# Transposing the fifth token tile's probabilities on TensorE in an attention and mixture-of-experts kernel

## The chip, the cores and the metric

One core of a Trainium2 chip runs the whole kernel. The metric is device time in microseconds, the median of several runs. The engines named here are TensorE (PE in the profile; PEld is its weight load), VectorE (DVE), ScalarE (ACT) and SyncE (SP). SyncE issues every DMA of this kernel, transposing ones too, in one queue.

## The reference

Attention with a learned bias that depends on position, and behind it a mixture of eight experts whose gate is balanced by eight Sinkhorn steps:

```python
B, H, S, D = (4, 8, 576, 64)              # E, DM, F = 8, 512, 1024
scores = q @ k^T / sqrt(D) + bias          # bias: [H, S, S], from positions
attn = exp(scores - max); attn = attn / (sum(attn) + 1e-9)
x = (attn @ v), heads side by side         # [2304, 512]
P = exp(x @ w_gate - max), then 8 times: rows and columns normalised
out = sum over e of P[:, e] * (relu(x @ w1[e]) @ w2[e])
```

## The kernel before

**Two stages.** In the first, attention runs, together with the first expert's products on those rows of x that are done; in the second, the other experts. Both write their instructions into a planner (class `Plan`) which gives each a cost, puts them into an order for each engine by a list schedule, and emits them. A DMA transpose has costs of its own in it (`transfer`, L206). Every instruction of the first stage shows line 202, the place where recorded instructions are issued, so the profile tells them apart by tile names.

**Units.** The attention works on 16 units, each of one batch and two heads. The 576 tokens of a head are cut into four tiles of 128 and a rest of 64; the rests of both heads share one tile, the unit's fifth token tile. A unit so has 9 score tiles of 128 x 576: two for each of four 128-token tiles, and one for both heads' rest. They go in five steps: four of two tiles each (`gi` 0 and 1, `hh` 0 and 1), and one step of a single tile (`gi` 2).

**A step.** `scores` multiplies q and k into a PSUM tile `ps_s` (tag s, two of them, 1024 float32 columns or two banks each). `st_max` on VectorE adds the bias, writes `sb` and takes the maximum. `st_exp` on ScalarE makes the exponentials and their sums, `st_rcp` the reciprocals. The probabilities are written as two float16 parts: `st_hi` (ScalarE) writes the high part of `ah`, `st_lo` (VectorE) the low part. `ah` is 128 x 1152 for one score tile, 128 x 2304 for two, and there are two `ah` buffers. Then `ah` is transposed, block of 128 x 128 by block, into `aT`: 18 blocks for a step of two tiles (tag aT, three buffers), 9 blocks for the fifth tile's step (tag aT4, one buffer). Before the change, `st_lo` ends in one DMA transpose, whatever the step:

```python
sync.dma_start_transpose(out=s["aT"], in_=ah.rearrange("p n s -> p (n s)"))
```

`attend` multiplies `aT` with v into the PSUM tile pv two steps later (`LAG = 2`); ScalarE and VectorE cut the product into two float16 parts of x (xa, xb, xc).

**Around it.** One pass of the main loop records, in this order: the scores of step n + 1, the exponentials of step n, the maxima of step n + 1, the value products that are due, `st_hi` and `st_lo` of step n - 1, the hooks, and one or two pieces of the first expert (tile l). The hooks load and cut the q, k and v of units to come (nat, qk, vs) and load bias tiles (bt) for SyncE's queue. `u_trans` transposes q and k on TensorE (8 blocks, 8 blocks and 2 blocks a unit) through a PSUM tile of tag l1, and copies them out as qkT. PSUM has eight banks: four for the two score tiles, two for l1, one each for l2 and pv.

Of the kernel before, what the change touches and what calls it, by code (L numbers as in the profile page):

```python
# [9 lines left out]
F16 = mybir.dt.float16  # L10
# [8 lines left out]
P = 128  # L19
# [243 lines left out]
def attention_sinkhorn_moe(ctx, tc, q, k, v, w1, b1, w2, wg, m1, m2, xm, xm4, xf, sel, out):  # L263
# [11 lines left out]
    plan = Plan()  # L275
    vec, act, pool, pe, sync = (
        Engine(plan, e, n)
        for e, n in ((nc.vector, "dve"), (nc.scalar, "act"), (nc.gpsimd, "pool"), (nc.tensor, "pe"), (nc.sync, "dma"))
    )
# [15 lines left out]
    id16 = consts.tile([P, P], F16, name="id16")  # L295
# [109 lines left out]
    with ExitStack() as actx:  # L405
# [35 lines left out]
        def ps_s():  # L441
            return psA.tile([P, 1024], F32, name="ps_s", tag="s", bufs=2)
# [68 lines left out]
        for kind in range(1, 4):  # L511
            vec.scalar_tensor_tensor(
                out=wr,
# [8 lines left out]
            out=wa.rearrange("p g (j k) -> p (g j) k", j=4),  # L522
# [88 lines left out]
        def bias_step(between=()):  # L611
# [27 lines left out]
            out=w1r, in0=pw[:, H : H + 2], scalar1=s_wb[:, 0:1], scalar2=2.0**-11, op0=ALU.mult, op1=ALU.mult  # L639
# [5 lines left out]
            out=w2m,  # L645
# [22 lines left out]
        for i in range(2):  # L668
            r = slice(32 * i, 32 * i + 1)
# [122 lines left out]
        with plan.urgent():  # L792
# [6 lines left out]
            out=c8, in0=u_qk[:, 0:1], scalar=0.125, in1=u_qk[:, 1:2], op0=ALU.mult, op1=ALU.mult  # L799
# [7 lines left out]
            out=g, in0=g0, scalar=s_qk[:, 0:1], in1=s_qk[:, 1:2], op0=ALU.mult, op1=ALU.mult  # L807
# [140 lines left out]
        def st_lo(s):  # L948
            n, ah = len(s["sb"]), s["ah"]
            s["aT"] = wrk.tile([P, 9 * n, P], F16, name="aT", tag="aT" if n == 2 else "aT4", bufs=3 if n == 2 else 1)  # L950
            for i, sb in enumerate(s["sb"]):
                vec.scalar_tensor_tensor(
                    out=ah[:, i, S:],
                    in0=sb,
                    scalar=s["st"][:, 3, i : i + 1],
                    in1=ah[:, i, 0:S],
                    op0=ALU.mult,
                    op1=ALU.subtract,
                )
            sync.dma_start_transpose(out=s["aT"], in_=ah.rearrange("p n s -> p (n s)"))  # L960

        def attend(u, gi, ss):

# [158 lines left out]
        for n in range(NS + LAG + 1):  # L1122
# [19 lines left out]
            if 0 < n <= NS:  # L1142
                s = steps[n - 1]
                st_hi(s)
                st_lo(s)
                u, gi, hh = s["key"]
                groups.setdefault((u, gi), []).append(s)
                if gi == 2 or hh == 1:
                    due.append((n + LAG, u, gi, groups.pop((u, gi))))
# [19 lines left out]
        vec, act, pool, pe, sync = nc.vector, nc.scalar, nc.gpsimd, nc.tensor, nc.sync  # L1169
# [623 lines left out]
    for n, (e, b) in enumerate(seq):  # L1793
        r = visit[n]
# [94 lines left out]
```

## Time and profile before

| what | value |
|---|---|
| median of 3 runs | 1820.13 us |
| lowest and highest run | 1817.78 and 1821.13 us |
| profiled execution | 1816.04 us, span 1814.2 us |
| TensorE busy | 1678.9 us, 93% of the span |
| VectorE busy | 1481.0 us, 82% |
| ScalarE busy | 1089.9 us, 60% |
| DMA queue of SyncE | 306496 packets, 327.51 MB, 60.6% of 16 engines' span |

The profile is of one execution, and its times are counted from the start of its span. The shares are averages over both stages, which have different limits; the attention ends at about 540 us. A wait is put down to whatever released it last.

### The profile page before, as it was taken

The page shows a single profiled execution, that of the slowest core. Times are in us where ns is not written, and L with a number is a line of the kernel's source. Part 1 is how long each engine was busy: PE and PEld are TensorE (multiplying, and loading weights), DVE is VectorE, ACT ScalarE, POOL GpSimd, SP SyncE. Part 2 cuts the span into 40 slices and gives each one's busy share as a digit, 9 for nine tenths or more (in the row PEclk, how much of TensorE's full clock was granted, in tenths as well). Part 3 has the DMA queues.
Part 4 walks back from the last instruction along what each step waited for, and adds up shares of the span by engine and source line. Part 5 has one row for each costly group of instructions (what it writes and reads, how often), then busy time and mean ns, then how long its engine had stood idle before and what let it go on. Part 6 is the DMA issues. An engine that isn't in the chain of part 4 may idle for free.

```text
span 1814.2 us, 40312 instructions
## 1 busy us (share of the span) xinstructions
PE 1678.9 (93%) x16574; PEld 1372.1 (76%) x16574; DVE 1481.0 (82%) x2748; ACT 1089.9 (60%) x1930; POOL 1.5 (0%) x10
## 2 busy tenths in 40 slices
PE   7777598899889899789999999999999999999998
PEld 4444355565566688678898898889888988898887
DVE  7999889888868788868887888778788879886666
ACT  7787678888856755555655555455556455453443
POOL 0000000000000000000000000000000000000000
PEclk9998699899999999899999999999999999999999
DMA  8768998999994234574565448455644564463321
GB/s 277 245 164 189 241 196 192 210 197 216 195 242 174 75 117 174 179 263 162 171 213 204 158 166 289 141 198 195 236 152 165 200 213 144 163 238 112 93 83 36
DMA packets 306680, 330.07 MB, mean 182 GB/s; under 512 B 191680, under 2 KB 234432, under 8 KB 301504
## 3 DMA queue, kind: packets, MB, share of 16 engines
q1 hardware_dynamic: 306496, 327.51, 60.6%
q8 instruction: 129, 2.11, 0.5%
q14 instruction: 55, 0.45, 0.1%
HBM read 195.72 MB, written 88.08 MB: 156 GB/s over the span
## 4 chain that ended last, share of the span: by engine, by line
PE 75%; DVE 10%; DMA 7%; ACT 2%; issue 2%; SPq 2%; DVEq 0%; ACTq 0%
PE bankA L1519 17%; PE bankA L1539 13%; PE bankB L1539 9%; PE bankE L1519 9%; PE bankE L1539 9%; PE l L202 5%; PE bankB L1519 4%; PE pv L202 3%; PE s L202 3%; DMA aT<-ah 2%; PE bankA L385 2%; SPq L202 2%; DVE area L202 1%; DVE sb L202 1%; DVE ah L202 1%
## 5 line engine op out<-in xcount | busy, mean ns | idle before, releaser
L1519 PEld LDWEIGHTS <-slot 128*128 128x128 f16 x5040 | 452.4, 98 | 65.3 <-issue 18.1
L1539 PEld LDWEIGHTS <-hA 128*128 128x128 f16 x2268 | 222.4, 98 | 33.8 <-issue 5.0
L202 PEld LDWEIGHTS <-area 128*128 128x128 f16 x2477 | 153.1, 99 | 108.0 <-issue 38.0
L1519 PE MATMUL bankE<-xt,slot 128*128 128x256 f16 (+1 forms) x1680 | 188.7, 264 | 10.8 <-ACT xt L1355 7.8
L1519 PE MATMUL bankA<-xt,slot 128*128 128x256 f16 (+1 forms) x1680 | 185.9, 262 | 0.4 <-ACT u L1576 0.4
L1564 ACT ACTIVATE hA<-c 128x512 f16<-128x512 f32 x189 | 117.9, 627 | 106.5 <-DVE c L1197 105.9
L1539 PEld LDWEIGHTS <-area 128*128 128x128 f16 x1512 | 148.0, 98 | 18.8 <-issue 1.4
L1539 PEld LDWEIGHTS <-hS 128*128 128x128 f16 x1512 | 147.7, 98 | 19.0 <-ACT hS L1564 1.3
L1197 DVE SCALAR_TENSOR_TENSOR hA<-c,hA 128x512 f16<-128x512 f32 x189 | 127.2, 684 | 11.5 <-ACT hA L1564 9.4
L202 DVE SCALAR_TENSOR_TENSOR ah<-sb,st,ah 128x576 f16<-128x576 f32 x144 | 113.1, 812 | 21.0 <-ACT ah L202 20.5
L1623 ACT COPY u<-bankA 128x512 f32<-128x512 f32 (+1 forms) x70 | 37.9, 542 | 153.5 <-PE bankA L1539 153.4
L202 ACT ACTIVATE ah<-sb,st 128x576 f16<-128x576 f32 x144 | 105.5, 771 | 28.4 <-DMA aT<-ah 23.0
L202 ACT ACTIVATE sb<-sb,st 128x576 f32<-128x576 f32 x144 | 110.5, 769 | 16.9 <-DVE st L202 16.6
L1576 ACT ACTIVATE u<-bankA 128x512 f32<-128x512 f32 x126 | 75.1, 596 | 73.7 <-PE bankA L1519 69.2
L202 PE MATMUL l<-area 128*128 128x512 f16 x413 | 110.0, 387 | 6.5 <-ACT area L202 2.2
L1197 DVE SCALAR_TENSOR_TENSOR acc<-c,fs,acc 128x256 f32<-128x256 f32 x252 | 110.1, 478 | 1.7
L202 PE MATMUL s<-qkT 128*128 128x512 f16 (+3 forms) x560 | 84.9, 306 | 24.6 <-DVE st L202 19.8
L1539 PE MATMUL bankB<-area,hA 128*128 128x256 f16 x756 | 90.8, 277 | 4.8 <-DVE area L1197 4.8
L1539 PE MATMUL bankA<-area,hA 128*128 128x256 f16 x756 | 88.4, 273 | 1.8 <-ACT hA L1564 1.4
L1539 PE MATMUL bankA<-area,hS 128*128 128x256 f16 x756 | 88.4, 273 | 1.4 <-ACT hS L1564 1.0
L1539 PE MATMUL bankA<-area 128*128 128x256 f16 x756 | 88.2, 273 | 1.0 <-ACT u L1623 1.0
L1539 PE MATMUL bankB<-area 128*128 128x256 f16 x756 | 88.5, 273 | 0.0
(228 smaller groups left out, 3090.2 us busy)
## 6 DMA issues: line engine op xcount, KB each, us to landing
sc_w<-stage SPq DMA_DIRECT2D x84, 512.0 KB, 3.1
acc<-sc_y SPq DMA_DIRECT2D x102, 256.0 KB, 4.0
area<-sc_w SPq DMA_DIRECT2D x48, 512.0 KB, 4.4
sc_y<-acc SPq DMA_DIRECT2D x84, 256.0 KB, 2.3
bt<-sc_bias SPq DMA_DIRECT2D x32, 576.0 KB, 4.7
xt<-sc_t SPq DMA_DIRECT2D x18, 1024.0 KB, 4.9
slot<-sc_w SPq DMA_DIRECT2D x36, 512.0 KB, 5.3
raw<-in_moe_w_dram SPq DMA_DIRECT2D x28, 512.0 KB, 4.9
```

The lines of the kernel that those rows point to most:

```text
L202: self.plan.record(self.name, cost, lambda: fn(*args, **kw), ins, outs, move)
L385: pe.matmul(ps[:, :512], h[:, a, ft, j * P : (j + 1) * P], w[:, wl, c : c + 512], start=(ft == 0 and i == 0), stop=(ft == 7 and i == 2),)
L1197: vec.scalar_tensor_tensor(out=o, in0=x, scalar=s, in1=y, op0=op0, op1=op1)
L1519: pe.matmul(ps[:, jf * w : jf * w + w], t[:, a, c * 512 + f * P : c * 512 + f * P + P], x(xp, c), start=(first and jf == 0 and c == 0 and ...
L1539: pe.matmul(ps[:, j * 256 : j * 256 + 256], h[:, a, fc * w + j * P : fc * w + j * P + P], t[:, wp, fc * 256 : fc * 256 + 256], start=(firs ...
L1564: on_act(0.58, lambda: act.activation(h[:, 0, sl], x, AF.Relu if relu else AF.Copy), [r], wk)
L1576: on_act(0.55, lambda: act.activation(tmp[k], bank[b], f, scale=HS), [b], [k], 0)
L1623: on_act(0.27 * nt, lambda: act.copy(tmp[k][:, :n], bank[b][:, :n]), [b], [k], 0)
```

## The change

The fifth token tile's step (`n == 1` score tile) no longer ends in a DMA transpose. Nine TensorE transposes write its blocks into a PSUM tile taken from the two score tiles (tag s, read as float16), recorded in the planner as one piece of work, and ScalarE copies them out to `aT`. The steps of two score tiles keep their DMA transpose.

```diff
@@ -957,7 +957,14 @@
                     op0=ALU.mult,
                     op1=ALU.subtract,
                 )
-            sync.dma_start_transpose(out=s["aT"], in_=ah.rearrange("p n s -> p (n s)"))
+            if n == 2:
+                sync.dma_start_transpose(out=s["aT"], in_=ah.rearrange("p n s -> p (n s)"))
+                return
+            ps = ps_s().bitcast(F16)[:, : 9 * P].rearrange("p (r x) -> p r x", x=P)
+            with plan.as_one():
+                for r in range(9):
+                    pe.transpose(ps[:, r], ah[:, 0, r * P : (r + 1) * P], id16)
+            act.copy(s["aT"], ps)
 
         def attend(u, gi, ss):
```

## Rows read from the trace of the kernel before

**Rows 1.** Busy time by stretch, one row a stretch, columns named in the first line

```profile
core 0: us, PE busy (x) PEld busy (x) DVE busy (x) ACT busy (x) POOL busy (x), PEclk, DMA share, GB/s
70.00:230.00 160.00, 112.06 (x1341) 67.53 (x1342) 147.45 (x303) 120.67 (x233) 0.00 (x0) 0.85 0.82 199
230.00:510.00 280.00, 254.52 (x2466) 162.66 (x2465) 245.51 (x598) 227.90 (x462) 0.00 (x0) 0.96 0.98 201
540.00:1814.20 1274.20, 1234.76 (x11641) 1090.35 (x11637) 1013.85 (x1706) 672.71 (x1106) 0.00 (x0) 0.99 0.48 169
```

**Rows 2.** Chain of waits from 230 to 510 us, shares by line

```profile
by line: PE l L202 29.9%; PE pv L202 15.5%; DMA aT<-ah 10.7%; PE s L202 9.7%; SPq L202 7.5%; issue 4.1%; DMA nat<-in_k_dram 4.0%; DVE ah L202 3.7%; DVE sb L202 3.2%; DMA nat<-in_q_dram 2.0%; ACT ah L202 1.4%; DVE area L202 1.2%; DVE qkT L20
```

**Rows 3.** Chain in order of time, start and length: two of ten transfers, and the end

```profile
286.28 6.41 DMA aT<-ah
...
478.54 2.40 DMA nat<-in_q_dram
...
504.74 6.08 DMA aT<-ah
...
535.67 4.33 PE bankS L1253 x169
```

**Rows 4.** DMA view from 230 to 510 us

```profile
DMA packets 139343, 56.37 MB, mean 201 GB/s; under 512 B 129072, under 2 KB 133936, under 8 KB 139312
...
q1 hardware_dynamic: 139312, 55.96, 97.3%
...
aT<-ah SPq DMA_TRANSPOSE x60, 5.1
```

**Rows 5.** All instructions on the tile aT, from issue to landing

```profile
DMA to landing us min/median/max: 3.2/5.0/8.5
```

**Rows 6.** SyncE's issues in order of time: start, length

```profile
316.40 2.71 SPq L202 DMA_TRANSPOSE aT<-ah  x1
...
319.83 1.32 SPq L202 DMA_TRANSPOSE aT<-ah  x1
...
460.58 1.69 SPq L202 DMA_TRANSPOSE aT<-ah  x1
...
464.36 3.92 SPq L202 DMA_TRANSPOSE aT<-ah  x1
```

**Rows 7.** Waits from 70 to 540 us: total us, times, longest

```profile
PEld L202 <- issue: 118.2, 254, 3.6
PE s L202 <- DVE st L202: 33.6, 30, 3.5
ACT ah L202 <- DMA aT<-ah: 23.0, 19, 3.0
DVE ah L202 <- ACT ah L202: 20.5, 20, 2.6
ACT sb L202 <- DVE st L202: 16.6, 20, 2.0
DVE sb L202 <- PE s L202: 12.1, 12, 1.9
```

**Rows 8.** TensorE transposes of q and k: all of them, and one group

```profile
L202 PE MATMUL l<-id,qk x288: 216/219/314, 63.1 to 489.3; 128*128 128x128 f16 x144
...
331.26 0.62 PE L202 MATMUL l<-id,qk 128*128 128x128 f16 x8 [1.98 <-DVE qk L202]
```

**Rows 9.** ScalarE copies out of PSUM by shape, up to 540 us

```profile
L202 ACT COPY qkT<-l 128x1024 f16<-128x1024 f16 x14 | 14.0, 999 | 2.9 <-PE l L202 2.7
...
L202 ACT COPY qkT<-l 128x256 f16<-128x256 f16 x14 | 5.1, 363 | 1.1 <-PE l L202 1.0
```

**Rows 10.** Two score tiles on TensorE, and one tile's maximum on VectorE

```profile
462.74 1.15 PE L202 MATMUL s<-qkT 128*128 128x512 f16 x8
...
460.47 0.81 DVE L202 CUSTOM_DVE_ANT_0 sb<-s,bt,sms 128x576 f32<-128x576 f32 x1
```

## The prediction

> **What bounds the kernel now.** I first read the busy times by stage, to see where the change can act [rows 1]. Up to 540 us the attention runs, and from there the experts. The fifth tiles all lie in the first part; in the second TensorE is busy 1234.76 of 1274.20 us and its order of work is planned by itself, so whatever the attention ends earlier or later moves the end by the same amount. I found no other way for the change to reach the second part.
>
> In the steady part of the attention (230 to 510 us) nothing is clearly the bound: of 280 us TensorE is busy 254.52, VectorE 245.51, ScalarE 227.90, and the DMA share is 0.98 [rows 1]. From 70 to 230 us VectorE leads with 147.45 of 160. So I went to the chain of waits for 230 to 510 us [rows 2]. TensorE's three lines there make 29.9 + 15.5 + 9.7 = 55.1%. Transfers make 10.7 (landing of transposes) + 4.0 + 2.0 (loads of k and q) = 16.7%, which is 46.8 us, and SP's own issuing 7.5%, 21 us. ScalarE's only line there of any size is 1.4%. The chain changes hands all the time: TensorE for some 10 us, then a late transfer, then TensorE again. Ten transfers carry the 46.8 us [rows 3]; the reader is to see that such a piece is either a transpose that took 6 us from issue to landing, or a load that SP issued late.
>
> Next the DMA view of the same stretch: the packets fill 97.3% of the 16 engines' time, 129072 of 139343 packets are under 512 bytes, and 60 transposes were issued [rows 4]. Sixty transposes are twelve units of five: 48 of 18 blocks of 128x128 and 12 of 9 blocks, 972 blocks. At 128 rows a block that is 124416 packets, which accounts for most of the small ones: the transposes fill the DMA engines in this stretch. A transpose takes 3.2 us to land at best, 5.0 at the median and 8.5 at worst [rows 5].
>
> **What is removed.** Sixteen transposes of 9 blocks. On SP such an issue takes 1.32 us in one place and 1.69 in another, against 2.7 to 3.9 of an 18-block one [rows 6]; 1.5 us x 16 = 24 us of SP's queue and, at half of what a large one costs, about as much of the DMA engines. Behind each stand in SP's queue the bias loads (bt) and the loads of q, k and v; when SP reaches the transpose before VectorE has written the tile's low part, they wait too. After the change SP comes to them at once. The fifth tile's ah buffer also comes free when TensorE has read it, not when a transfer has landed. ScalarE waits 23.0 us in 19 places for a transpose to release ah [rows 7], and the transposes of the chain end in that wait or in that of the value products. What is late next: the 64 large transposes, which stay.
>
> What this is worth has to be bounded. Above: 24 us, if the DMA engines are the true bound and every freed microsecond shortens the stage. Below: nothing, since none of the ten transfers on the chain is itself shown to be a 9-block one, so what helps is only that the others find a shorter queue. In between, in proportion: the twelve small ones are 108 of 972 blocks, or 108 x 128 = 13824 of 139343 packets, 10%; 10% of the 46.8 + 21 us on the chain is 7 us. I take more than that, because what a queue that is 97% full costs is mostly waiting: the median landing stands 1.8 us above the best. If the ten chain pieces lose half of this, they lose 9 us; with 10% of SP's 21 us (2 us) and an estimated 1 us in the stretches before and after, it is 12 us.
>
> **What is added.** TensorE: nine transposes for each of 16 tiles. The kernel has such a group already, eight transposes of the q and k parts in 0.62 us [rows 8]; nine are 0.70 us, and 16 groups 11.2 us. Below, nothing (all inside idle time, of which TensorE has 25 us in 230 to 510 us); above, 11.2 us. I take its share of the chain, 55%: 6.2 us. A single transpose of the group shows 219 ns in the trace, but they overlap: eight in 0.62 us is 78 ns each, and that is what the queue behind them sees [rows 8]. The Trainium skill, TensorE: Matmul & The Clock Gate, Part 4: PE-mode transpose, speaks against the change here: it gives about 275 ns for one in a kernel's context, which one after the other would be an estimated 2.5 us a tile and 40 us in all, and the sum below would be -12 + 22 + 0.7 = +11 us. The trace agrees with the size of one and not with their coming one after the other, so this stands among the rivals with a small chance.
>
> ScalarE: one copy of 1152 columns out of PSUM. The 1024-column copy takes 0.999 us and the 256-column one 0.363 [rows 9], so 0.83 ns a column and 1.10 us here, 17.7 us over 16 tiles. Its cover is ScalarE's idle time, 52 us in 230 to 510 us; it appears on the chain with a few per cent, I take 4%, so 0.7 us. Without the cover it would cost the 17.7. Behind a copy that waits for its transposes stand the exponentials of the next step on ScalarE, and VectorE's low part waits for those in turn.
>
> VectorE gets nothing. The landing tile aT4 has one buffer, but its reader of the unit before is a whole unit, 23 us, older, so I expect no wait there. The planner gets other costs and may order all engines differently; that I can only cover by the range.
>
> The change moves a wait: TensorE now comes to the tile's transposes in its fixed order and waits for VectorE's low part if that is late, with scores and expert pieces queued behind. And it takes one of the two score tiles in PSUM (tag s) for the transposes and the copy, at least 0.70 + 1.10 = 1.8 us a unit, in which the next scores have one place only. Below, nothing: two score tiles take TensorE 1.15 us together, and each takes VectorE 0.81 us [rows 10], nine tiles in a unit's 280/12 = 23 us, so the places are mostly not short. Above, 1.8 x 16 = 29 us. I take nothing, since today's wait of TensorE for VectorE at the scores comes in 30 places for 144 tiles, 33.6 us in all [rows 7].
>
> **Sum.** -12 + 6.2 + 0.7 = -5 us. The profiled execution took 1816.04 us (span 1814.2), 4.1 us under the median of 1820.13, so by it the kernel would take 1811, and as a median 1815 us. A change of 0.2%, 3.6 us, is about what the runs of this kernel can tell from none.
>
> **Rivals.**
> First, that it cancels. The transfers give back only in proportion (7 us), and TensorE and ScalarE take 6.9: 1820 us. For it: TensorE, not DMA, holds more than half of the chain. Against it: a nearly full queue.
>
> Second, that the score tile decides, and the kernel gets slower. Place: scores that wait for the copy of the transposed tile, and VectorE's max step (the line that writes sb) behind them. If half of the 29 us lands on the chain, -5 + 14.5 gives 1830 us, and all of it 1844. It decides from 5/16 = 0.3 us of stall a unit on. For it: TensorE waiting at scores for VectorE is the longest wait for another engine in the list, and VectorE already waits 12.1 us for scores [rows 7]. Against it: those waits are at the same rotation of two tiles and yet small.
>
> Third, that TensorE becomes the bound: the 11.2 us come in full, with 0.7 for ScalarE, against 7 from the transfers: 1825 us. For it: 254.52 of 280 us busy, and pieces of the expert products are always ready to fill it, so idle time is rare. Against it: TensorE does have 25 idle us there, and the chain leaves it for transfers ten times.
>
> Fourth, that the new transposes do not overlap and come at the 219 ns that a single one shows: 9 x 0.219 x 16 = 31.5 us, 17.3 of them on the chain, so -12 + 17.3 + 0.7 = +6, 1826 us. Against it: the group of eight that the rows show ran as one [rows 8]. The page named above leads to this rival.
>
> **Chances and range.** My forecast 0.45, cancelling 0.23, the score tile 0.18, TensorE 0.11, no overlap 0.03. So faster 0.45, the same 0.23, slower 0.32. The forecast's own range is 1802 (all 24 us of transfers given back, 6 taken: -18) to 1816. The range to hold 8 in 10 has to reach over both signs: 1802 to 1833, the upper end a little past half of the score tile's price.
>
> **What would show it.** After the change the trace should have 64 transposes on SP, 144 more transposes on TensorE, 16 ScalarE copies of 1152 columns at 1.1 us; a DMA share in the steady stretch nearer 0.9 than 0.97; a median landing nearer 4 than 5 us; ScalarE's wait for ah well under 23 us; and the gate's first products (bankS, now at 535.67 us [rows 3]) some 5 us earlier, with the experts' part unchanged in length. I am wrong if the landing times stay where they are (the DMA engines were full only by name), if TensorE's wait at scores grows by more than 5 us, or if waits of ScalarE or TensorE for the new tile appear that together pass 10 us.

## The result: slower by half a per cent

| kernel | median | runs | ratio to before, 95% interval |
|---|---|---|---|
| before | 1821.13 us | 5 | |
| changed | 1828.09 us | 5 (1827.01 to 1833.14) | 1.0052 (1.0036 to 1.0068) |

The changed kernel is 0.36 to 0.68% slower, 9.5 us at the middle of the interval; the two medians are 7.0 us apart. The forecast was 5 us faster. The profiled execution of it has a span of 1826.0 us, 11.8 more than the one of before.

Where the time went is seen in two views. The chain in order of time has the gate's first products (bankS) at 546.28 us, against 535.67 before [rows 3]: 10.6 us, nearly all of the difference, are lost before the attention ends. A large transpose near its end is on the chain as before, for 8 us.

```profile
503.23 8.05 DMA aT<-ah
...
545.48 0.80 PE pv L202 x28
546.28 4.51 PE bankS L1260 x176
```

The busy times by stretch (columns as in [rows 1]) show that the DMA engines are relieved and that only ScalarE is fuller: over the same 280 us the DMA share is 0.88 instead of 0.98, VectorE has done 5 us less, TensorE as much, ScalarE 6 us more.

```profile
230.00:510.00 280.00, 253.92 (x2525) 164.78 (x2523) 240.57 (x583) 233.75 (x461) 0.00 (x0) 0.96 0.88 185
```

The DMA view of 230 to 510 us and the landing of all transposes on aT, to be held against [rows 4] and [rows 5]:

```profile
DMA packets 120182, 51.77 MB, mean 185 GB/s; under 512 B 109654, under 2 KB 114774, under 8 KB 120150
...
q1 hardware_dynamic: 120150, 51.34, 86.9%
...
DMA to landing us min/median/max: 4.5/5.2/9.1
```

The packets went down by more than the tenth expected, partly because the stretch holds less work now. But the transposes land no sooner. The 5.0 us of before mixes two shapes: counted apart in that trace, the 16 small ones landed in 3.2 us at best and 3.3 at the median, the 64 large ones in 4.55 at best and 5.16 at the median. The large ones of the changed kernel have 4.54 and 5.21. SP's issue of them is long (3.36 us at the median before, against 1.32 of a small one), and in both shapes the landing follows the end of the issue by some 1.9 to 2.0 us at the median.

The new operations, by tile and by form: the 144 transposes, the 16 copies with the idle time in front of them, and one tile in order of time (468.50 + 1.12 = 469.62, so the score tile was held 1.83 us: from the first transpose into it to the end of the copy out of it).

```profile
L202 PE MATMUL s<-id,ah x144: 219/219/311, 201.7 to 539.3; 128*128 128x128 f16 x144
...
L202 ACT COPY aT<-s 128x1152 f16<-128x1152 f16 x16 | 17.8, 1113 | 4.4 <-PE s L202 4.2
...
467.79 0.67 PE L202 MATMUL s<-id,ah 128*128 128x128 f16 x9
...
468.50 1.12 ACT L202 COPY aT<-s 128x1152 f16<-128x1152 f16 x1
```

Their sizes are as forecast (0.70 and 1.10 us). The waits from 70 to 555 us, beside [rows 7]:

```profile
PE s L202 <- DVE st L202: 37.0, 39, 4.9
DVE ah L202 <- ACT ah L202: 30.1, 23, 3.2
ACT ah L202 <- DMA aT<-ah: 23.6, 18, 2.9
...
DVE sb L202 <- PE s L202: 10.1, 16, 1.8
...
ACT aT L202 <- PE s L202: 4.2, 6, 1.5
```

ScalarE's wait for a transpose to give ah back, which should have shrunk, is 23.6 us (23.0 before). What has grown by some 10 us is VectorE's wait for ScalarE's high part, 20.5 to 30.1 us. I took that as a first hint that the copy stands in the way on ScalarE; but it is 27.9 us in the first run below, which has no such copy on the chip, so by itself it shows nothing. TensorE waits for ah at the new transposes, 2.2 + 1.9 + 1.6 + 1.4 = 7.1 us in four rows further down this list, where it waited 0.2 us for ah before.

### The profile page after: what moved, and what is told of

Same layout as the page of the kernel before. It is cut to its first block, busy times and chain, and to the rows that moved or that the text cites. A ratio compares the mean times of both kernels' runs of the same rounds, so it can differ in the third digit from the quotient of the medians.

```text
span 1826.0 us, 40560 instructions
## 1 busy us (share of the span) xinstructions
PE 1691.0 (93%) x16718; PEld 1380.7 (76%) x16718; DVE 1481.7 (81%) x2748; ACT 1105.3 (61%) x1946; POOL 1.5 (0%) x10
## 4 chain that ended last, share of the span: by engine, by line
PE 75%; DVE 12%; DMA 5%; issue 3%; ACT 2%; SPq 0%; DVEq 0%; ACTq 0%
PE bankA L1526 17%; PE bankA L1546 13%; PE bankB L1546 9%; PE bankE L1546 9%; PE bankE L1526 9%; PE l L202 5%; PE bankB L1526 4%; PE s L202 3%; DMA aT<-ah 3%; PE pv L202 2%; DVE sb L202 2%; PE bankA L385 2%; DVE ah L202 2%; DVE area L202 2%; DVE sms L202 1%
## 5 line engine op out<-in xcount | busy, mean ns | idle before, releaser
L1526 PE MATMUL bankE<-xt,slot 128*128 128x256 f16 (+1 forms) x1680 | 189.5, 265 | 11.2 <-ACT xt L1362 7.8
L1546 PEld LDWEIGHTS <-area 128*128 128x128 f16 x1512 | 148.2, 98 | 18.8 <-issue 1.4
L202 DVE SCALAR_TENSOR_TENSOR ah<-sb,st,ah 128x576 f16<-128x576 f32 x144 | 113.3, 812 | 30.5 <-ACT ah L202 30.1
L1204 DVE SCALAR_TENSOR_TENSOR hA<-c,hA 128x512 f16<-128x512 f32 x189 | 127.2, 684 | 11.8 <-ACT hA L1571 9.8
L202 ACT ACTIVATE ah<-sb,st 128x576 f16<-128x576 f32 x144 | 105.6, 772 | 31.6 <-DMA aT<-ah 23.6
L1546 PE MATMUL bankE<-area,hS 128*128 128x256 f16 x756 | 88.6, 273 | 2.9 <-ACT hS L1571 2.2
```

Source lines behind the costliest of these rows:

```text
L202: self.plan.record(self.name, cost, lambda: fn(*args, **kw), ins, outs, move)
L1204: vec.scalar_tensor_tensor(out=o, in0=x, scalar=s, in1=y, op0=op0, op1=op1)
L1526: pe.matmul(ps[:, jf * w : jf * w + w], t[:, a, c * 512 + f * P : c * 512 + f * P + P], x(xp, c), start=(first and jf == 0 and c == 0 and ...
L1546: pe.matmul(ps[:, j * 256 : j * 256 + 256], h[:, a, fc * w + j * P : fc * w + j * P + P], t[:, wp, fc * 256 : fc * 256 + 256], start=(firs ...
```

## The experiments

All ratios are to the kernel before on the same chip. Intervals are mostly about 0.12% on either side, 2 us. To add things up I take ratio times 1819 us; a difference of two kernels is so known to about 3 us. Apart from the second run, every kernel here is planned anew, so its order differs as well; what that can do by itself is seen in the first five runs.

**Three theories at first**: the work itself; the PSUM score tile that is shared; the planner's new order of everything.

*Order.* The same instructions as before, in the order of the changed kernel:

```diff
-            with plan.as_one(): ... pe.transpose(...)
-            act.copy(s["aT"], ps)
+            plan.node("pe", 9 * P / 2350, lambda: nc.sync.dma_start_transpose(out=dst, in_=src), [ah, id16], [ps, aT])
+            plan.node("act", 0.13 + 9 * P * 0.00097, lambda: None, [ps], [aT])
```

> The planner is given the nodes of the changed kernel (nine transposes on TensorE into a score tile, a copy on ScalarE), but what is emitted at the transposes' place is the DMA transpose of before; so the instructions are those of before in the order of the changed kernel. Theory work (the loss of about 7 us is what TensorE, ScalarE and the waits around the new transposes take): 1821 us, as before. Theory score tile (the PSUM score tile is held by transposes and copy): 1821 as well, since nothing holds it on the chip. Theory order (the planner's new order of all engines costs it, whatever the work): 1828.

Measured 1831.42 us, 1.0065 (1.0052 to 1.0078). This is what the theory of the order expected, and 3 us more. I saw a cause of its own in the trace: this order reckons with an ah that comes free early, while the chip still transposes by DMA, and ScalarE waits 37.8 us for ah, where the kernel before and the changed one both have 23 to 24. That this wait costs the 12 us is not shown: the run with 0.16 us a block below has 34.7 us of it and is 2.9 us slower than before.

```profile
ACT ah L202 <- DMA aT<-ah: 37.8, 31, 4.3
```

So it decides nothing alone. The opposite: order of before, work of the changed kernel.

```diff
+            if n == 1:
+                plan.small[len(plan.nodes)] = (ah[:, 0, :], s["aT"])
             sync.dma_start_transpose(out=s["aT"], in_=ah.rearrange("p n s -> p (n s)"))
...
+            if i in self.small:          # in emit, in place of the DMA
+                move(free_score_tile, src)   # nine transposes; the copy follows 0.95 later
```

> The opposite of the first run: the planner is given the kernel of before, with its DMA transposes, and its order is kept on every engine (VectorE's is that of before word for word); only at emission each 9-block transpose is replaced by the nine TensorE transposes, into whichever score tile is free at that place, and by ScalarE's copy 0.95 planner microseconds later. Theory work: 1828, as the changed kernel. Theory score tile: 1821 to 1824, as the tile is taken only where it is free. Theory order: 1821 or less, down to 1814 by the 6 us that the removal of the transposes alone gave.

Measured 1834.68 us, 1.0085 (1.0072 to 1.0098). None of the three theories expected as much. With the order of before kept, the new work put in at these places costs 15 us, 6 more than where the planner puts it; ScalarE waits 13.4 us for the transposes here, against 4.2 in the changed kernel. So the loss does not need the new order. And small changes of the order move little, as three kernels show in which one number of the planner's model is changed (`0.165 * out.free_size()` in `transfer`):

> The kernel of before with one number of the planner's model changed, a transposed block at 0.16 instead of 0.165 us; the work is the same, the order differs at about as many places on VectorE (300 lines) as between before and the changed kernel (376). Theory order: the time moves by several us, 1815 to 1828 and more likely up, as the constants were chosen for this order. Theories work and score tile: 1821, within 3 us.

Measured 1822.21 us, 1.0016 (1.0005 to 1.0028).

> As the run with 0.16, with 0.17 us a block. Same expectations: theory order 1815 to 1828, theories work and score tile 1821 within 3 us.

Measured 1820.18 us, 1.0005 (0.9996 to 1.0013).

> The changed kernel with 0.16 us a block in the planner's model. Theory order: several us from 1828 either way, so that it may even meet before. Theories work and score tile: 1828 within 3 us.

Measured 1828.62 us, 1.0053 (1.0039 to 1.0068), the changed kernel's time. As the sole cause the order falls: the loss comes without the new order, and these three changes of order move a kernel by 3 us at most. That the order has a part in it stays open, as the first run, with nothing but the order changed, was 11.8 us slower than before.

*Which part of the work.* First nothing but the removal, then the transposes without the copy (a fill of aT at the first unit stands in for what is left out):

```diff
-            ps = ps_s()...; nine pe.transpose; act.copy(s["aT"], ps)
+            if s["key"][0] == 0: pool.memset(s["aT"], 0.0)
```

> The fifth tile is not transposed at all: its aT keeps zeros from one fill at the first unit, so the fifth tile's output rows are left out. No DMA transpose, no TensorE transposes, no copy. My prediction had the removal alone at -12 us (0 to -24): 1809. If the large transposes do not land sooner for it, as the trace of the changed kernel suggests (median landing 5.2 us against 5.0), it is 0 to -4: 1817 to 1821. Theory order: anywhere within some 8 us of before.

Measured 1813.09 us, 0.9963 (0.9950 to 0.9975): -6.7 us. The landing of the remaining transposes is that of the 64 large ones before (5.16 us at the median), so the gain does not come from there.

```profile
DMA to landing us min/median/max: 4.6/5.1/9.0
...
by line: PE l L202 31.8%; DMA aT<-ah 23.3%; PE pv L202 15.5%; PE s L202 10.0%; issue 4.7%; DVE ah L202 4.1%; DVE sb L202 3.5%; ACT ah L202 1.9%; DMA bt<-sc_bias 1.8%; DVE qk L202 0.9%; DVE st L202 0.9%; DVE qkT L202 0.5%; DVE vs L202 0.5%; 
```

The second line is the chain from 230 to 510 us, to be held against [rows 2]. SP's issuing (7.5%) and the loads of k and q (6.0%) are off it, as the prediction meant, but the landing of transposes has grown from 10.7 to 23.3% of it: with the bias loads, SP and transfers have 25.1% of the chain, and 24.2% before. So the waits have changed places more than gone, in this chain at least, and by which path the 6.7 us come is not shown.

> As the changed kernel without ScalarE's copy out: the fifth tile's aT keeps zeros, so its output rows are left out. The transposes on TensorE stay. Theory work, if ScalarE's 16 x 1.12 us carry it: 1820 or less; if TensorE carries it: 1827. Theory score tile: the tile is held 0.7 instead of 1.8 us a unit, so most of the 7 us go: 1822. Theory order: anywhere within some 8 us.

Measured 1817.97 us, 0.9991 (0.9977 to 1.0004). Against the run without transposes TensorE's 16 groups, with the short hold of the score tile that goes with them, cost 0.9991 - 0.9963 = 0.28%, 5.1 us; the copy, up to 1.0052, costs 0.61%, 11 us.

*Another PSUM tile.* Eight blocks and one block through tag l1, two ScalarE copies:

```diff
-            ps = ps_s().bitcast(F16)[:, : 9 * P]...
+            for r0, nr in ((0, 8), (8, 1)):
+                ps = psA.tile([P, 1024], F16, name="ps_t", tag="l1", bufs=2)...
```

> As the changed kernel, but the transposes go through the two PSUM tiles of tag l1 that the q and k transposes use (eight blocks and one block, two copies on ScalarE), so the score tiles stay free for scores. Theory score tile: the loss goes, 1821 or less. Theory work: 1828, or 2 to 4 us more for the second copy's fixed cost (16 x 0.25 us) and waits at l1.

Measured 1836.68 us, 1.0098 (1.0075 to 1.0121). In this form a half-finished product of the first expert in l1 is overwritten, so part of its result is changed. It is inconclusive on the score tile: leaving the score tiles alone did not help, but l1 has users of its own that wait, and there are two copies.

*What of the copy costs.* Its time in ScalarE's queue, the hand-over (ScalarE waiting in order for TensorE), or the hold of the score tile? ScalarE's copy alone, from ah, with no transposes:

```diff
-            ps = ...; nine pe.transpose; act.copy(s["aT"], ps)
+            act.copy(s["aT"].rearrange("p n x -> p (n x)"), ah[:, 0, :])
```

> The changed kernel with the transposes left out, and ScalarE copying the 1152 columns of ah straight to aT: the fifth tile is not transposed, so its output rows are left out. It is the run without any transpose (1813) plus ScalarE's 16 copies alone, with no PSUM and no TensorE in them. Theory ScalarE (the copy's time in ScalarE's queue, 16 x 1.1 to 1.3 us, costs about 10 us): 1823. Theory score tile (what costs is that the copy holds the PSUM tile): 1814. Theory hand-over (what costs is that ScalarE waits in order for TensorE, and what follows waits with it): 1815.

Measured 1818.44 us, 0.9996 (0.9987 to 1.0006), 6.0 us over the run without any transpose. (This copy waits for VectorE's low part of ah, 3.2 us in seven places.) The hand-over with almost no time on ScalarE:

```diff
-            act.copy(s["aT"], ps)
+            act.copy(s["aT"][:, :, 0:1], ps[:, :, 0:1])
```

> The changed kernel whose ScalarE copy takes one column of each block (9 of 1152): the fifth tile's output rows are left out. The wait of ScalarE for TensorE stays, its time falls from 1.12 to some 0.2 us and the score tile is held about 0.9 us less. It stands beside the run without the copy (1818) and the changed kernel (1828). Theory ScalarE: 1819. Theory hand-over: 1825 to 1828. Theory score tile: 1822.

Measured 1817.95 us, 0.9993 (0.9983 to 1.0004), as without a copy. ScalarE waits 5.1 us for TensorE in nine places here, and that costs nothing that can be measured; the copy's length does, by ScalarE's time or by the hold. On VectorE:

```diff
-            act.copy(s["aT"], ps)
+            vec.tensor_copy(s["aT"], ps)
```

> The changed kernel with the copy on VectorE instead of ScalarE, about 0.75 us each, 12 us in all on the engine with the least idle time. Theory ScalarE: 1820 to 1824, as ScalarE is free of it and VectorE's 12 us are partly covered. Theory score tile: 1826, as it is held only some 0.35 us less. Theory hand-over: 1828 or more, as VectorE waits in its place.

Measured 1818.79 us, 1.0000 (0.9991 to 1.0008): 9.5 us better than on ScalarE, on the engine that is the busier one. Its busy times by stretch, its copies, and its waits:

```profile
230.00:510.00 280.00, 254.31 (x2562) 166.51 (x2562) 253.76 (x607) 230.36 (x462) 0.00 (x0) 0.96 0.93 191
...
L202 DVE COPY aT<-s x16: 748/758/759, 206.9 to 533.3; 128x1152 f16<-128x1152 f16 x16
...
ACT ah L202 <- DMA aT<-ah: 15.1, 18, 3.1
DVE ah L202 <- ACT ah L202: 11.4, 12, 3.4
```

VectorE's wait for ScalarE's high part is 11.4 us, where it was 20.5 before and 30.1 with the copy on ScalarE: VectorE spends 12 us on copies and gets 9 of waiting back. That is not the whole account: the same list has it waiting 4.7 us for the transposes and 16.9 for scores, 12.1 before. The copy late, at the planner's lowest priority:

```diff
+            plan.prio = 2
             act.copy(s["aT"], ps)
+            plan.prio = 1
```

> The changed kernel with the copy given the planner's lowest priority, so that it goes where ScalarE has nothing else ready in the model; the score tile is held longer. Theory ScalarE: the same 17.9 us but in gaps, 1821 to 1825. Theory hand-over: 1820, as the transposes are long done when ScalarE comes to the copy. Theory score tile: over 1830.

Measured 1837.56 us, 1.0104 (1.0091 to 1.0118), 9.5 us worse than the changed kernel. Its timeline has the transposes at 380.25 us and their copy at 386.95; the score tile is held to 388.06, 7.8 us, and VectorE's maxima wait for scores one at a time.

```profile
380.25 0.67 PE L202 MATMUL s<-id,ah 128*128 128x128 f16 x9
...
386.95 1.11 ACT L202 COPY aT<-s 128x1152 f16<-128x1152 f16 x1
...
391.15 0.82 DVE L202 CUSTOM_DVE_ANT_0 sb<-s,bt,sms 128x576 f32<-128x576 f32 x1 [1.56 <-PE s L202]
```

The waits of this kernel say the same: VectorE for scores 34.0 us, against 12.1 before [rows 7].

```profile
DVE sb L202 <- PE s L202: 34.0, 38, 2.9
```

*Hold and ScalarE's time apart.* The long hold with the copy of one column a block:

```diff
+            plan.prio = 2
             act.copy(s["aT"][:, :, 0:1], ps[:, :, 0:1])
+            plan.prio = 1
```

> As the run with the copy of one column a block (1818), but at the lowest priority: the score tile is held long (about 8 us, as in the low-priority run at 1837) while ScalarE works only 0.2 us a tile. The fifth tile's output rows are left out. If the hold is what costs: 1830 to 1837. If it is ScalarE's time: 1818 to 1822.

Measured 1829.29 us, 1.0053 (1.0039 to 1.0067): the late copy costs 10.9 us over the one-column run, with no more time on ScalarE. Summed over the 16 tiles in the two timelines, the score tile is held 108 us here and 20 us there; 88 us more for 10.9, or 0.12 us lost for each us held. The low-priority run against the changed kernel gives the same (115 us against 35, for 9.5). That all of it is the hold is argued, not shown: VectorE waits 24.0 us for scores, 15.1 with one column, but aT comes late as well, and ScalarE waits 23.9 us for value products (xa, xb, xc, vs), 14.4 with one column. The short hold with ScalarE's time:

```diff
             act.copy(s["aT"][:, :, 0:1], ps[:, :, 0:1])
+            act.copy(s["sb"][0].bitcast(F16), ah[:, 0, :])
```

> As the run with the copy of one column a block, and right behind it ScalarE copies the 1152 columns of ah into the dead score buffer sb: ScalarE's time of the changed kernel (about 1.3 us a tile), a hold of 1.1 us as in the one-column run. The fifth tile's output rows are left out. If ScalarE's time is what costs: 1825 to 1828, as the changed kernel. If the hold: 1818 to 1820.

Measured 1825.00 us, 1.0030 (1.0016 to 1.0044): 0.37% or 6.7 us over the one-column run, for 16 copies of 1.15 us. The hold came out a little longer than meant, 24 us in all against 20, which at 0.12 is half a us.

```profile
L202 ACT COPY sb<-ah x16: 1132/1152/1156, 202.3 to 538.8; 128x1152 f16<-128x1152 f16 x16
```

Last, the copy shared between two engines, as the version that might have beaten both:

```diff
-                    pe.transpose(ps[:, r], ...)
-            act.copy(s["aT"], ps)
+                    pe.transpose(ps[:, r if r < 4 else r + 4], ...)
+            act.copy(s["aT"][:, 0:4], ps[:, 0:4])
+            vec.tensor_copy(s["aT"][:, 4:9], ps[:, 8:13])
```

> The changed kernel with the blocks put into the tile's two banks, four copied by ScalarE (about 0.57 us) and five by VectorE (about 0.45 us) side by side. If ScalarE's time and the hold both count, half of the 10 us go on either account: 1820 to 1823. If VectorE's time is really free, as the copy on VectorE suggests, 1819 or a little less.

Measured 1824.80 us, 1.0024 (1.0014 to 1.0035), between the copy on ScalarE and the one on VectorE. But it did not do what it was built for: in all 16 tiles the two copies run one after the other, and ScalarE waits 14.5 us in 13 places for VectorE's copy into the same aT. The score tile is held 34 us in all, as in the changed kernel, so a copy shared side by side is untested.

```profile
418.62 0.49 DVE L202 COPY aT<-s 128x640 f16<-128x640 f16 x1
419.15 0.58 ACT L202 COPY aT<-s 128x512 f16<-128x512 f16 x1 [1.54 <-DVE aT L202]
```

Over all these runs, in several orders, the five kernels with the full copy by ScalarE out of PSUM lie at 1.0052 to 1.0104 (one of them the run through l1, in two copies), and the three without it, with one column of it or with it on VectorE at 0.9991 to 1.0000. No version was found that beats the kernel before; the room for one is small, since the transposes on TensorE take 5.1 of the 6.7 us that the removal gives.

## Why the prediction was wrong, by its own steps

The measured 1828.09 us lies inside the stated range, 1802 to 1833, but on the other side of the kernel before than the forecast: the removal gave less than its term, and the copy and the hold of the score tile cost more than theirs.

| term | forecast | measured | from |
|---|---|---|---|
| removal of 16 DMA transposes | -12 | -6.7 | run without any transpose |
| TensorE's 16 groups | +6.2 | +5.1 | transposes without the copy, short hold included |
| ScalarE's copy, time in its queue | +0.7 | +6.0, +6.7 | copy without transposes; second copy beside one column |
| hold of the score tile by the copy | 0 | about +2, an estimate | tile held 35 us in all, 15 more than with one column, at 0.12 |
| sum | -5 | +9.5 measured whole | |

The steps together give -6.7 + 5.1 + 6.7 + 2 = +7, and 2 of the 9.5 us stay without a place; that is within what these differences can tell, each of them known to about 3 us and made between kernels of different order.

**The step that failed first is ScalarE's share.** I priced the copy by ScalarE's small share of the chain, 4% (no row gives that figure; its line there has 1.4%), and by its idle time, 52 us. It costs about a third of its time, +6 to +6.7 us where I had +0.7. Why, the chain does not show. My reading is that ScalarE's high part of ah is what VectorE's low part waits for, and behind that the large transpose, so that what delays ScalarE comes out under VectorE's and DMA's names. The wait of VectorE for ScalarE rose with ScalarE's time (17.3 us with no transpose, 23.1 with the copy alone, by the waits of those two traces) and fell to 11.4 when VectorE did the copy. But it was no longer in the run with the second copy than with one column (18.8 and 19.4 us), and it was 27.9 and 26.3 us in two kernels without any copy (the order of the changed kernel; 0.16 us a block). So this loop is an argument that the waits do not bear out, and the path stays open; that ScalarE's time costs 6 to 7 us is shown by the two runs that add it without a longer copy out of the score tile.

**The removal was oversized.** What left the queue was as I had estimated: SP's 16 issues took 22.3 us in all (24 forecast), and the time of the queue's packets fell from 60.6% of 1814.2 us to 59.5% of 1811.3, about 22 us of 16 engines. But it gave 6.7. The proportional value that I had worked out, 7 us, meets that number; by which path, the runs do not show, so the agreement may be luck. The addition for shorter landings was wrong. It rested on 3.2 us as the best landing, which was a half-size transpose's; the large ones of before stood 0.6 us above their own best, not 1.8, and five of the ten chain pieces to which I applied it are loads and not transposes. With the small ones gone, and with no transpose of the fifth tile at all, the median is 5.1 to 5.2 us and the best 4.5 to 4.6: taking work off a DMA queue that was 97% full did not bring the large ones down sooner.

**TensorE's term was right**, in size (0.67 us a group against 0.70) and, as far as 3 us can tell, in what it cost (5.1 against 6.2). The fourth rival falls: a transpose shows 219 ns, and nine of them take 0.67 us. The Trainium skill, TensorE: Matmul & The Clock Gate, Part 4: PE-mode transpose, gives about 275 ns for one in a kernel; the trace has 219, and that figure is not what a group costs per block.

**The rivals.** The first, cancelling at 1820, had the right price for the removal and 6.9 us for what is added, where the runs have 5.1 + 6.7 + 2. The second, the score tile, came out on the right side and near the right time, 1830, but by the wrong share, so its time is luck: a late copy with its long hold costs 10.9 us, yet at 2.2 us a unit the hold is the smaller part. The third, TensorE as the bound at 1825, is near the time too, and wrong: TensorE's groups cost 5.1 us and not 11.2. No rival had ScalarE's queue, though the prediction itself names what stands behind the copy there: exponentials, and VectorE's low part after them.

**The signs.** The smaller DMA share came, and the experts' part kept its length (1278.5 us from the gate's first products to the end, now 1279.7); the shorter landing, the shorter wait for ah and the earlier gate did not. Of the three signs of being wrong, the landing stayed, as named. TensorE's wait at scores grew by 3.4 us, less than the 5 named. The waits for the new tile came to 4.2 us on ScalarE and 7.1 on TensorE, 11.3 together, past the 10 named; but the run with one column has 5.1 and 4.8 of them and is as fast as before, so they are not what costs.

## What to carry to other kernels

An engine's idle time and its share of the chain said little here about what more work on it costs: 18 us on ScalarE with 52 us idle cost 6 to 7, while 12 us on the busier VectorE cost nothing that can be measured. Where two engines can do the work, both are worth a run. Before the best value of a duration is taken as what a row could fall to, it should be seen whether the shapes are mixed in it. And where an operation takes a turn in a rotation of two buffers, it should be watched how long it holds its buffer: the copy at low priority, in otherwise idle time, held the score tile three times as long, and that kernel is one of the two slowest measured here. Last, a wait that has grown with a change names its cause only when the same wait is read in a kernel without the part that is suspected: here it was nearly as long without any copy.

## What was not expected of the hardware

Two things. The landing of an 18-block transpose stayed at 5.2 us at the median (5.16 and 5.21) while the share of the DMA engines fell from 97.3% to 86.9%, so the high share did not mean that a transpose would land sooner with less in the queue. And the same 1152 columns of float16 out of PSUM took VectorE 0.758 us and ScalarE 1.113 us.
